# Around a one-slot expert stage: weights before squares, relu rows in buffers of their own, two conversions and one scale moved

## The chip, the core and the metric

The kernel runs on one core of a Trainium2 chip. The metric is the device time of one execution in microseconds (us). Five engines run side by side, each through its own instruction list in order: TensorE (PE, matrix products and transposes; PEld is its weight load), VectorE (DVE), ScalarE (ACT), GpSimd (POOL) and SyncE (SP, which here only issues DMAs). They wait for one another through semaphores.

## What is computed

Causal attention with a decay over 4 x 8 heads of 576 rows gives 2304 tokens of 512 numbers. Each token goes to one of eight experts (two matrices with a relu between), its row is scaled by a gate, and a dense layer pair with a softplus between follows for all tokens.

```
out[mask] = gate_w[mask, None] * (np.maximum(x[mask] @ w1[e], 0.0) @ w2[e])     # for each expert e
h = x @ w_in
g = np.maximum(h, 0.0) + np.log1p(np.exp(-np.abs(h)))
return g @ w_out
```

## The kernel before

After the attention (to about 240 us) and the routing (to about 280 us) come nine expert stages, in the order of `ORDER`: three-slot stages `t`, two-slot stages `b` and the only one-slot stage `s`. A slot is 128 token rows of one expert. The text numbers the stages 0 to 8; stage 5 is `("t", 1)`, **stage 6 is `("s", 0)`**, stages 7 and 8 are `("t", 2)` and `("t", 3)`. Then comes the dense layer pair (`ffn`).

**Weights.** A stage uses eight pieces of weights of 512 KB; W6[4] is piece 4 of stage 6. Pieces 0 to 3 serve the first product of a stage (L1149, in stage 6 L1219), 4 to 7 the second (L1129), whose eight blocks `fb` = 0 to 7 use one half piece each. `wsplit` handles a piece: an SP DMA into a buffer `raw` of the pool `stage` (four buffers in all), ACT writes the high part `wh` (L1040), DVE the low part `wl` (L1041). `feed(ph, want)` does one missing piece of the current stage, or, when that has all eight, pieces of the next stage until it has `want`. A DMA of a piece is issued when the `raw` that was handed out four before it has been read by DVE.

**Dense conversions.** `conv.step()` loads 512 KB of the dense weights through the same four `raw` buffers, in fixed order, and DVE turns them in three instructions (L1417 to L1419); an ACT square (L1426) follows later. The table `STEPS` says behind which of a stage's 16 blocks (eight of the first product, eight of the second) a step stands.

**Rows.** `xslot` makes the next stage's token columns: four PE transposes into one of two PSUM banks, ACT `xh` (L1086), DVE `xl` (L1087); in stage 6 it stands behind `fb` 1, 3 and 5 for the three slots of stage 7. At a stage's end `scatter` has ACT write the result row `y` (L1116, three buffers) and POOL scatter it by DMA; `square` (L1104, ACT) takes its sum of squares. In stage 6 (`small`) ACT writes relu rows `hs` (L1223), which before the change take a buffer of `y`; `turn` transposes `hs`, ACT writes `hh` (L1232) and DVE `hl` (L1233).

**The dense pair.** It goes over five chunks of rows, chunk 0 of 512 rows first, in 16 steps each; `n` counts all steps. In step n PE does the first product of step n and the second product of step n-3. DVE does `e`, `e` of step n-1, `r` and `u` of n, then `gl` of n-1 (L1542, L1543, L1528, L1530, L1549); POOL does one subtraction (L1531) between `u` and the next `e`. Behind odd n up to 13 one dense piece is split (ACT L1434, DVE L1435). In chunk 0 the scale of the later chunks is found: `total` (DVE, `y_m` and `y_mb`), `add` (one PE product, L1460), then `find` and `scale(1)` (nine small DVE instructions, L1464 to L1484). `rows.prep` makes the columns of chunk 1 with that scale: four PE transposes (L1378) into the only bank T, ACT high part, DVE low part (L1380).

Of the kernel before, what the change touches and what calls it, by code (L numbers as in the profile page):

```python
# [9 lines left out]
F32 = mybir.dt.float32  # L10
# [16 lines left out]
DM = H * D  # L27
# [8 lines left out]
ROWS = "tbs"  # L36
NG = 9
STEPS = {0: "0101010010101010", 1: "0001000001000000", 2: "0001000001000000", 3: "0001000001000000", 4: "0001000001000000",
         5: "0101010010101000", 7: "0101010010101000", 8: "1110110000000000"}
STEPS = {ph: [x == "1" for x in s] for ph, s in STEPS.items()}  # L40
SPLITS = [(0,), (1, 2), (3, 4), (5,), (6,), (7,), (), ()]
ORDER = [("t", 0), ("b", 0), ("b", 1), ("b", 2), ("b", 3), ("t", 1), ("s", 0), ("t", 2), ("t", 3)]
# [1 line left out]
NMAIN = len(SLOTS)  # L44
# [4 lines left out]
WROW = 528  # L49
# [839 lines left out]
def compact(tc, g, p, ps):  # L889
    nc = tc.nc  # L890
    V = nc.vector
    x = 0
    tok, flag = (p.tile([128, NMAIN], dt, name=nm, bufs=1) for nm, dt in (("ptok", F32), ("pflag", BF16)))
    kept = p.tile([128, NMAIN], F32, name="pkept", bufs=1)
    V.tensor_copy(g.tok, g.gidx)
    while x < NMAIN:
        m, y = SLOTS.index(PLACES[x]), 1
        while x + y < NMAIN and m + y < NMAIN and SLOTS[m + y] == PLACES[x + y]:
            y += 1
        V.tensor_copy(tok[:, x:x + y], g.tok[:, m:m + y])  # L900
        V.tensor_copy(kept[:, x:x + y], g.pv[:, 0, m:m + y])
        x += y
    V.scalar_tensor_tensor(flag, tok, float(KEPT), kept, op0=ALU.is_lt, op1=ALU.mult)
    V.tensor_tensor(kept, kept, flag, op=ALU.subtract)
    V.tensor_tensor(tok, tok, g.dmf, op=ALU.subtract)
    V.tensor_tensor(tok, tok, kept, op=ALU.mult)
    V.tensor_tensor(tok, tok, g.dmf, op=ALU.add)
    yield
    n = ps()[:, 0:NMAIN]
    nc.tensor.matmul(n, g.onesm, flag, start=True, stop=True)  # L910
    sums = p.tile([128, NMAIN], F32, name="sums", bufs=1)
    V.tensor_tensor_scan(sums, g.onesm[:, 0:NMAIN], n, 0.0, op0=ALU.mult, op1=ALU.add)
    first = p.tile([128, 1], F32, name="first", bufs=1)
    V.tensor_scalar(first, sums[:, NMAIN - 1:NMAIN], -1.0, float(KEPT), op0=ALU.mult, op1=ALU.add)
    V.tensor_tensor(sums, sums, n, op=ALU.subtract)
    V.tensor_scalar(sums, sums, g.row, first, op0=ALU.add, op1=ALU.add)
    V.tensor_tensor(sums, sums, g.dmf, op=ALU.subtract)
    V.tensor_tensor(sums, sums, flag, op=ALU.mult)
    V.tensor_tensor(g.sidx, sums, tok, op=ALU.add)
    a = p.tile([128, NMAIN], I32, name="batch", bufs=1)  # L920
    gate_rows(V, g.grow, g.gidx, a)
# [54 lines left out]
def experts(tc, g, w1, w2, win, wout, out):  # L976
# [4 lines left out]
    phases = list(ORDER)  # L981
    n_ph = len(phases)
    with ExitStack() as both, ExitStack() as ctx:
# [5 lines left out]
        yp = g.yp = pool("e_y", 3)  # L989
# [4 lines left out]
        hp = pool("e_h", 4, ctx)  # L994
# [137 lines left out]
        def wide(ph):  # L1132
            w = WIDTH[phases[ph][0]]
            n = 128 * w
            last = ph == n_ph - 1
            xh, xl = (t.rearrange("p c a n -> p c (a n)") for t in X.pop(ph))
            hts = []
            for gg in range(4):
                hh = hp.tile([128, 2, n], F32R, name="hh", tag="hh")
                hl = hp.tile([128, 2, n], F32R, name="hl", tag="hl")  # L1140
                if w == 2:
                    pair = ps_h.tile([128, 2, n], F32, name="h", tag="h")
                for a in range(2):
                    pl = pair[:, a] if w == 2 else ps_h.tile([128, n], F32, name="h", tag="h")
                    fs = slice(128 * (2 * gg + a), 128 * (2 * gg + a) + 128)
                    for c in range(4):
                        wh, wl = W[ph][c]
                        for m, (x, y) in enumerate(((wh, xh), (wh, xl), (wl, xh))):
                            nc.tensor.matmul(pl, x[:, fs], y[:, c], start=(c == 0 and m == 0),  # L1149
                                             stop=(c == 3 and m == 2))  # L1150
                    if w == 2 and a == 0:
                        continue
                    src, to = (pair, slice(0, 2)) if w == 2 else (pl, a)
                    nc.scalar.activation(hh[:, to], src, ACTF.Relu)
                    nc.vector.scalar_tensor_tensor(hl[:, to], src, 0.0, hh[:, to].bitcast(F32), op0=ALU.max, op1=ALU.subtract)
                    if 2 * gg + a in (0, 2, 6):
                        feed(ph, 0)
                    if STEPS[ph][2 * gg + a]:
                        conv.step()
                    if ph == 0 and (gg, a) == (0, 0):  # L1160
                        gates(tc, g, g.lt)
                    if ph == 0 and (gg, a) in ((1, 1), (3, 0)):
                        if gg == 1:
                            store_gates(tc, g, hp, bank)
                        next(places, None)
                hts += [(hh[:, a], hl[:, a]) for a in range(2)]
                if w == 2 or gg == 0:
                    feed(ph, 0)
                square()
                if gg == 0 and ph == n_ph - 2:  # L1170
                    conv.powers["i"].total(g.wsq[:, 0], ALU.add)
                if gg == 3 and last:
                    rows.powers[0].total(g.ysq, ALU.max)
            if last:
                for a in range(SIZES[0]):
                    rows.load(0, a)
            py = [ps_y.tile([128, DM], F32, name="y", tag="y") for _ in range(w)]
            for fb in range(8):
                l2(ph, py, hts[fb], fb, range(w))
                xnext(ph, fb)  # L1180
                if fb and not last:
                    feed(ph, min(fb, 4))
                if fb == 1:
                    ggather(ph)
                if not last and STEPS[ph][8 + fb]:
                    conv.step()
                if ph == n_ph - 2 and fb == 2:
                    conv.powers["i"].add(bank()[:, 0:1])
                if ph == n_ph - 2 and fb == 3:
                    conv.powers["i"].find()  # L1190
                if last:
                    if fb == 0:
                        conv.square(0)
                    if fb == 1:
                        conv.powers["o"].total(g.wsq[:, 1], ALU.add)
                    if fb == 2:
                        rows.powers[0].add(bank()[:, 0:1])
                        rows.powers[0].find()
                    if 3 <= fb < 3 + SIZES[0]:
                        rows.prep(0, fb - 3, bank)  # L1200
                    for x in SPLITS[fb]:
                        conv.split("i", x // 2, x % 2)
                    if fb == 5:
                        conv.powers["o"].add(bank()[:, 0:1])
                        conv.powers["o"].find()
                    if fb == 7:
                        conv.split("o", 0, 0)
            for a in range(w):
                scatter(ph, a, py[a])

        def small(ph, after1=None):
# [7 lines left out]
                    nc.tensor.matmul(pl, x[:, c], w[:, fs], start=(c == 0 and m == 0), stop=(c == 3 and m == 2))  # L1219

            def relu(pl):
                hs = yp.tile([128, WROW], F32, name="hs", tag="y")[:, 0:DM]
                nc.scalar.activation(hs, pl, ACTF.Relu)  # L1223
                return hs

# [16 lines left out]
            pl = ps_h.tile([128, 512], F32, name="h", tag="h")  # L1242
            for c in range(4):
                half_mm(pl, 0, c)
            while squares:
                square()
            h0 = relu(pl)
            next_weights(0)
            next_weights(0)
# [13 lines left out]
            for fb in range(8):  # L1263
                l2(ph, py, hts[fb], fb, [0])
                if fb == 0 and not after1:
                    hts += turn(h1)
                if main and fb % 2:
                    xnext(ph, fb // 2)
                if fb < 4:
                    next_weights(fb + 1)  # L1270
                if fb == 2 and main:
                    ggather(ph)
# [214 lines left out]
def ffn(tc, g, conv, rows, square, out):  # L1487
# [4 lines left out]
    with ExitStack() as ctx:  # L1492
# [91 lines left out]
        for n in range(len(units) + 3):  # L1584
# [14 lines left out]
                conv.split("o", *late[n])  # L1599
            if n < 3:  # L1600
                square()
            if n == 5:
                rows.powers[1].total(g.ysq, ALU.max)
            if n == 7:
                rows.powers[1].add(bank()[:, 0:1])
                rows.powers[1].find()
                scale(1)
            if n >= 3:
                l2(*units[n - 3])
            if n < len(units) and c + 1 < NC:  # L1610
                for a in range(SIZES[c + 1]):
                    if fb == (1 + 2 * a if c else (6, 7, 8, 11)[a]):
                        rows.load(c + 1, a)
                    if fb == (3 + 2 * a if c else (9, 11, 12, 14)[a]):
                        rows.prep(c + 1, a, bank)


# [33 lines left out]
```

## Time and profile before

| quantity | value |
|---|---|
| median of three runs | 915.23 us (914.03 to 915.61) |
| the profiled execution, its own time | 914.66 us |
| its span, first to last instruction | 912.9 us |
| mean granted TensorE clock | 0.981 |
| busy: PE, DVE, ACT, POOL | 858.8, 702.2, 565.0, 378.9 us |
| stage 5, stage 6, stages 7 and 8 begin on PE | 396.8, 430.3, 449.5, 486.9 us |
| dense pair begins on PE | 523.8 us |

The times in the text are of the profiled execution, counted from the start of its span; 1.8 us of its own time lie outside the span. PE is the busiest engine, but its matmul ends are modelled, so what counts is where it sat idle and what ended the idle time.

### The profile page before, as it was taken

To read this page: it belongs to the slowest core of one execution; us is meant where nothing else is said; L and a number is where in the kernel's file an instruction comes from. 1 tells how busy PE (TensorE), PEld (TensorE's weight loads), DVE (VectorE), ACT (ScalarE), POOL (GpSimd) and SP (SyncE) were. 2 spreads that over 40 slices of the span, in tenths; PEclk is the share of its full clock that TensorE was granted. 3 is DMA by queue.
4 is the path that set the end of the run, shared out by engine and by line. 5 is a ranking of instruction groups with operands and counts; after the bars stand their busy time and mean duration, and the time that the engine had idled before them with its cause. 6 is when DMAs were issued, how large, how long until landed. Compare 5 with 4: busy or idle time off the path is not lost.

```text
span 912.9 us, 17317 instructions
## 1 busy us (share of the span) xinstructions
PE 858.8 (94%) x6298; PEld 595.7 (65%) x6298; DVE 702.2 (77%) x1541; ACT 565.0 (62%) x1052; POOL 378.9 (42%) x526
## 2 busy tenths in 40 slices
PE   2999999999649999999799999999999999999998
PEld 2888787887539998898598844444444444664443
DVE  3788888888678777776587867888878778777775
ACT  3788888788564666665655776655454554566453
POOL 6678677777252322423403043324222422334221
PEclk9999999999859999999999999999999999999999
DMA  8776676691336878887767120101100200100001
GB/s 179 160 164 146 153 161 146 147 244 42 105 98 210 287 274 270 261 302 258 258 201 271 51 71 1 33 16 59 32 5 1 70 1 1 59 1 24 1 1 46
DMA packets 102814, 109.72 MB, mean 120 GB/s; under 512 B 62948, under 2 KB 72184, under 8 KB 102720
## 3 DMA queue, kind: packets, MB, share of 16 engines
q1 hardware_dynamic: 97282, 93.49, 36.4%
q0 software_dynamic: 5152, 14.87, 4.6%
q8 instruction: 51, 0.84, 0.4%
q14 instruction: 43, 0.35, 0.1%
q10 hardware_dynamic: 286, 0.17, 0.1%
HBM read 93.31 MB, written 15.20 MB: 119 GB/s over the span
## 4 chain that ended last, share of the span: by engine, by line
PE 52%; DVE 8%; POOL 3%; DMA 3%; ACT 3%; issue 2%; DVEq 0%; POOLq 0%; ACTq 0%
PE h L1517 14%; PE y L1562 11%; PE h L1149 11%; PE y L1129 10%; PE t L1562 4%; POOL e L1531 2%; DMA raw<-in_moe_w_dram 2%; DVE r L1528 2%; DVE e L1542 2%; DVE wl L1041 1%; DVE e L1543 1%; PE t L1085 1%; DVE dw L1435 1%; DVE u L1530 1%; ACT wh L1040 1%
## 5 line engine op out<-in xcount | busy, mean ns | idle before, releaser
L1531 POOL TENSOR_TENSOR e<-u,e 128x512 f32<-128x512 f32 (+1 forms) x80 | 103.8, 1297 | 245.2 <-DVE u L1530 241.9
L1527 ACT ACTIVATE e<-h,s_h 128x512 f32<-128x512 f32 (+1 forms) x80 | 51.2, 640 | 122.8 <-PE h L1517 122.7
L1562 PE MATMUL y<-dw,gh 128*128 128x512 f16 x448 | 111.4, 379 | 0.7 <-ACT ob L1570 0.7
L1549 DVE SCALAR_TENSOR_TENSOR gl<-e,s_gup,gh 128x512 f16<-128x512 f32 (+1 forms) x80 | 97.4, 1218 | 9.1 <-ACT gh L1547 8.7
L1562 PEld LDWEIGHTS <-gh 128*128 128x128 f16 x576 | 56.3, 98 | 66.2 <-ACT e L1529 1.0
L1041 DVE TENSOR_TENSOR wl<-raw,wh 128x1024 fp32r<-128x1024 f32 x64 | 77.8, 1223 | 21.3 <-ACT wh L1040 20.2
L1149 PE MATMUL h<-xh,wh 128*128 128x384 f32 (+1 forms) x256 | 80.3, 314 | 4.5 <-ACT xh L1086 3.3
L1149 PE MATMUL h<-xl,wh 128*128 128x384 f32 (+1 forms) x256 | 79.8, 312 | 0.9 <-DVE xl L1087 0.9
L1149 PE MATMUL h<-xh,wl 128*128 128x384 f32 (+1 forms) x256 | 79.9, 312 | 0.7 <-DVE wl L1041 0.7
L1528 DVE TENSOR_SCALAR r<-h,s_h 128x512 f32<-128x512 f32 (+1 forms) x80 | 55.6, 695 | 32.3 <-ACT e L1527 32.2
L1040 ACT ACTIVATE wh<-raw 128x1024 fp32r<-128x1024 f32 x64 | 67.0, 1055 | 21.5 <-DMA raw<-in_moe_w_dram 20.3
L339 DVE SCALAR_TENSOR_TENSOR pts<-pt,pts 128x512 f16<-128x512 f32 (+3 forms) x128 | 69.8, 567 | 11.9 <-ACT pts L336 11.2
L1517 PEld LDWEIGHTS <-wh 128*128 128x128 f16 x480 | 47.2, 99 | 47.4 <-issue 1.4
L1517 PEld LDWEIGHTS <-wl 128*128 128x128 f16 x480 | 47.1, 98 | 46.9 <-issue 0.8
L1547 ACT ACTIVATE gh<-e,s_gup 128x512 f16<-128x512 f32 (+1 forms) x80 | 53.6, 670 | 34.4 <-DVE e L1543 34.4
L336 ACT ACTIVATE pts<-pt 128x512 f16<-128x512 f32 (+3 forms) x128 | 58.5, 496 | 23.2 <-PE pt L349 11.1
L1129 PE MATMUL y<-wh,hh 128*128 128x512 f32 x168 | 67.8, 404 | 0.3 <-ACT hh L1232 0.3
L1542 DVE TENSOR_TENSOR e<-r,e 128x512 f32<-128x512 f32 (+1 forms) x80 | 50.4, 630 | 22.8 <-POOL e L1531 22.8
L313 ACT ACTIVATE p<-sm,mx 128x512 f32<-128x512 f32 (+3 forms) x128 | 67.9, 559 | 0.0
L1517 PE MATMUL h<-yth,wh 128*128 128x512 f16 x192 | 65.9, 384 | 0.0
L1129 PE MATMUL y<-wl,hh 128*128 128x512 f32 x168 | 65.7, 391 | 0.0
L1517 PE MATMUL h<-yth,wl 128*128 128x512 f16 x192 | 65.2, 380 | 0.0
(343 smaller groups left out, 2413.0 us busy)
## 6 DMA issues: line engine op xcount, KB each, us to landing
raw<-in_moe_w_dram SPq DMA_DIRECT2D x68, 512.0 KB
cb<-ncum SPq DMA_DIRECT2D x32, 288.0 KB
raw<-in_moe_w_in_dram SPq DMA_DIRECT2D x16, 512.0 KB
raw<-in_moe_w_out_dram SPq DMA_DIRECT2D x16, 512.0 KB
yg<-yd SPq DMA_DIRECT2D x18, 264.0 KB
cb<-ncum SPq DMA_DIRECT2D x32, 144.0 KB
qt<-in_q_dram SPq DMA_DIRECT2D x32, 128.0 KB
kt<-in_k_dram SPq DMA_DIRECT2D x32, 128.0 KB
```

The lines of the kernel that those rows point to most:

```text
L313: nc.scalar.activation(p[:, 0:n], s[:, 0:n], ACTF.Exp, scale=-1.0, bias=m)
L339: nc.vector.scalar_tensor_tensor(lo, ps, UP, hi, op0=ALU.mult, op1=ALU.subtract)
L1040: nc.scalar.activation(hi, r, ACTF.Copy)
L1041: nc.vector.tensor_sub(lo, r, hi.bitcast(F32))
L1129: nc.tensor.matmul(py[a], x[:, 128 * a:128 * a + 128], w[:, fb % 2], start=(fb == 0 and m == 0 and w is wh), stop=(fb == 7 and m == 1))
L1149: nc.tensor.matmul(pl, x[:, fs], y[:, c], start=(c == 0 and m == 0), stop=(c == 3 and m == 2))
L1517: nc.tensor.matmul(pl, w[:, fs], x[:, d], start=(d == 0 and m == 0), stop=(d == 3 and m == 2))
L1528: nc.vector.tensor_scalar(r, pl, back, 0.0, op0=ALU.mult, op1=ALU.max)
L1531: nc.gpsimd.tensor_sub(e, u, e)
L1542: nc.vector.tensor_sub(d, r, d)
L1549: nc.vector.scalar_tensor_tensor(gl, d, s, gh, op0=ALU.mult, op1=ALU.subtract)
L1562: nc.tensor.matmul(PO[c][a], x, w, start=(fb == 0 and m == 0 and w is wh), stop=(fb == FB - 1 and m == 1))
```

## The change

In stage 5 `feed` may go to six pieces of stage 6 instead of four, so W6[4] and W6[5] are split behind blocks 5 and 6 of stage 5, two blocks after W6[3]. In stage 6 `hs` gets two buffers of its own, and the three squares of stage 5's rows move from ahead of the first relu to behind blocks 5, 6 and 7. Of the dense conversions one leaves stage 5 (block 4 of its second product); stage 7 gets two more, behind the last two blocks of its second product; stage 8 has four (behind blocks 1, 3, 4 and 5 of its first product) where it had five (0, 1, 2, 4, 5). In the dense pair `total` moves from step 5 to 4, `add`, `find` and `scale(1)` from step 7 to 8, and the first `prep` of chunk 1 from step 9 to 10. `sums` reuses the tile `kept`.

```diff
 STEPS = {0: "0101010010101010", 1: "0001000001000000", 2: "0001000001000000", 3: "0001000001000000", 4: "0001000001000000",
-         5: "0101010010101000", 7: "0101010010101000", 8: "1110110000000000"}
+         5: "0101010010100000", 7: "0101010010101011", 8: "0101110000000000"}
...
-    sums = p.tile([128, NMAIN], F32, name="sums", bufs=1)
+    sums = kept
...
                 if fb and not last:
-                    feed(ph, min(fb, 4))
+                    feed(ph, min(fb, 6 if phases[ph + 1][0] == "s" else 4))
...
             def relu(pl):
-                hs = yp.tile([128, WROW], F32, name="hs", tag="y")[:, 0:DM]
+                hs = hp.tile([128, DM], F32, name="hs", tag="hs", bufs=2)
...
-            while squares:
-                square()
+            if not main:
+                while squares:
+                    square()
...
+                if main and fb > 4:
+                    square()
...
-            if n == 5:
+            if n == 4:
                 rows.powers[1].total(g.ysq, ALU.max)
-            if n == 7:
+            if n == 8:
                 rows.powers[1].add(bank()[:, 0:1])
                 rows.powers[1].find()
                 scale(1)
...
-                    if fb == (3 + 2 * a if c else (9, 11, 12, 14)[a]):
+                    if fb == (3 + 2 * a if c else (10, 11, 12, 14)[a]):
                         rows.prep(c + 1, a, bank)
```

The first place is ACT from the end of stage 5 to the end of stage 6 (`wh` is a weight piece, `y` and `junk,ysq` the result rows and their squares, `hs` the relu rows). Before:

```order
L1116 ACTIVATE y<-y,gsl 128x512 x3
L1104 ACTIVATE junk,ysq<-y 128x512 x3
L1223 ACTIVATE hs<-h 128x512
L1040 ACTIVATE wh<-raw 128x1024 x2
L1232 ACTIVATE hh<-t 128x512
L1040 ACTIVATE wh<-raw 128x1024
L1223 ACTIVATE hs<-h 128x512
L1040 ACTIVATE wh<-raw 128x1024
L1232 ACTIVATE hh<-t 128x512
L1040 ACTIVATE wh<-raw 128x1024
L1086 ACTIVATE xh<-t 128x4x128
```

And of the change, the same place:

```order
L1040 ACTIVATE wh<-raw 128x1024 x6
L1116 ACTIVATE y<-y,gsl 128x512 x3
L1223 ACTIVATE hs<-h 128x512
L1040 ACTIVATE wh<-raw 128x1024 x2
L1232 ACTIVATE hh<-t 128x512
L1223 ACTIVATE hs<-h 128x512
L1232 ACTIVATE hh<-t 128x512
L1040 ACTIVATE wh<-raw 128x1024
L1086 ACTIVATE xh<-t 128x4x128
...
L1104 ACTIVATE junk,ysq<-y 128x512 x3
```

Two `wh` have moved from between the relu rows to ahead of the `y` rows (six in a row now), and the three squares from ahead of the first `hs` to the end of the stage. DVE's `wl` and SP's DMAs move with the `wh`.

The second place is DVE at the border of stages 7 and 8 (`wl` a weight piece, `dw` a dense conversion of three instructions, `hl` the low part of a first product). Before, from the last `wl` of stage 7:

```order
L1041 TENSOR_TENSOR wl<-raw,wh 128x1024
L1417 TENSOR_SCALAR dw<-raw 128x512
L1418 SCALAR_TENSOR_TENSOR dw<-raw,dw 128x512
L1419 SCALAR_TENSOR_TENSOR dw<-raw,dw 128x512
L1155 SCALAR_TENSOR_TENSOR hl<-h,hh 128x384
L1041 TENSOR_TENSOR wl<-raw,wh 128x1024
L1417 TENSOR_SCALAR dw<-raw 128x512
L1418 SCALAR_TENSOR_TENSOR dw<-raw,dw 128x512
L1419 SCALAR_TENSOR_TENSOR dw<-raw,dw 128x512
L1155 SCALAR_TENSOR_TENSOR hl<-h,hh 128x384
L1417 TENSOR_SCALAR dw<-raw 128x512
```

And of the change (the lines below the edit bear numbers three higher):

```order
L1422 SCALAR_TENSOR_TENSOR dw<-raw,dw 128x512
L1420 TENSOR_SCALAR dw<-raw 128x512
L1421 SCALAR_TENSOR_TENSOR dw<-raw,dw 128x512
L1422 SCALAR_TENSOR_TENSOR dw<-raw,dw 128x512
L1420 TENSOR_SCALAR dw<-raw 128x512
L1421 SCALAR_TENSOR_TENSOR dw<-raw,dw 128x512
L1422 SCALAR_TENSOR_TENSOR dw<-raw,dw 128x512
L1155 SCALAR_TENSOR_TENSOR hl<-h,hh 128x384
L1041 TENSOR_TENSOR wl<-raw,wh 128x1024
L1155 SCALAR_TENSOR_TENSOR hl<-h,hh 128x384
L1420 TENSOR_SCALAR dw<-raw 128x512
```

Three conversions now stand ahead of the first `hl` of stage 8, where one stood, and none between its first and second `hl`, where one stood.

The third place is DVE in the dense pair, steps 7 and 8 of chunk 0 (`gl` closes a step; `y_b` to `s_o` are `find` and `scale(1)`; the `dw` split stands in odd steps). Before, the end of step 7:

```order
L1528 TENSOR_SCALAR r<-h,s_h 128x512
L1530 TENSOR_SCALAR u<-e 128x512
L1549 SCALAR_TENSOR_TENSOR gl<-e,s_gup,gh 128x512
L1435 SCALAR_TENSOR_TENSOR dw<-dw,o_up 128x1024
L1464 TENSOR_SCALAR y_b<-t 128x1
...
L1484 TENSOR_TENSOR s_o<-s_gdn,o_dn 128x1
L1542 TENSOR_TENSOR e<-r,e 128x512
```

And of the change, from the end of step 7 through step 8:

```order
L1552 SCALAR_TENSOR_TENSOR gl<-e,s_gup,gh 128x512
L1438 SCALAR_TENSOR_TENSOR dw<-dw,o_up 128x1024
L1545 TENSOR_TENSOR e<-r,e 128x512
L1546 TENSOR_TENSOR e<-e,v 128x512
L1531 TENSOR_SCALAR r<-h,s_h 128x512
L1533 TENSOR_SCALAR u<-e 128x512
L1552 SCALAR_TENSOR_TENSOR gl<-e,s_gup,gh 128x512
L1467 TENSOR_SCALAR y_b<-t 128x1
...
L1487 TENSOR_TENSOR s_o<-s_gdn,o_dn 128x1
L1545 TENSOR_TENSOR e<-r,e 128x512
```

The nine small instructions have moved from behind a split to behind the `gl` of a step without a split; `total` moves in the same way from step 5 to step 4.

## Rows read from the trace of the kernel before

**Rows 1.** PE's list of waits from stage 5 on: total, times, longest.
```profile
PE h L1149 <- DVE hl L1155: 1.0, 1, 1.0
...
PE t L1460 <- DVE y_mb L1456: 0.7, 1, 0.7
PE y L1562 <- ACT ob L1570: 0.7, 1, 0.7
```

**Rows 2.** Stretches: window, its length, busy by engine, granted clock, DMA.
```profile
451.10:454.50 3.40, 3.40 (x12) 3.40 (x12) 0.00 (x0) 0.00 (x0) 2.62 (x3) 0.50 0.86 322
...
587.60:591.00 3.40, 3.40 (x12) 1.42 (x10) 2.75 (x6) 1.93 (x3) 1.36 (x1) 0.50 0.02 6
```

**Rows 3.** PE timeline in stages 6 and 7: start, duration, idle before.
```profile
432.81 0.39 PE L1219 MATMUL h<-wh,xl 128*128 128x512 f32 x1
...
439.06 0.50 PE L1129 MATMUL y<-wh,hl 128*128 128x512 f32 x1 [0.83 <-DVE hl L1233]
...
449.48 0.44 PE L1149 MATMUL h<-xh,wh 128*128 128x384 f32 x1 [3.30 <-ACT xh L1086]
450.85 0.51 PE L1149 MATMUL h<-xl,wh 128*128 128x384 f32 x1 [0.93 <-DVE xl L1087]
```

**Rows 4.** ACT timeline in stage 6.
```profile
433.35 0.63 ACT L1104 ACTIVATE junk<-y 128x512 bf16<-128x512 f32 x1
...
434.47 0.60 ACT L1223 ACTIVATE hs<-h 128x512 f32<-128x512 f32 x1 [0.39 <-DMA yd<-y,sidx]
434.96 2.00 ACT L1040 ACTIVATE wh<-raw 128x1024 fp32r<-128x1024 f32 x2
...
445.59 1.06 ACT L1040 ACTIVATE wh<-raw 128x1024 fp32r<-128x1024 f32 x1 [1.44 <-DMA raw<-in_moe_w_dram]
```

**Rows 5.** DVE timeline in stage 6.
```profile
436.04 2.36 DVE L1041 TENSOR_TENSOR wl<-raw,wh 128x1024 fp32r<-128x1024 f32 x2 [6.80 <-ACT wh L1040]
...
450.11 0.68 DVE L1087 TENSOR_TENSOR xl<-t,xh 128x512 fp32r<-128x512 f32 x1
```

**Rows 6.** SP's DMA issues: W6[4] to W6[7], then W7[0] to W7[3].
```profile
423.40 6.24 SPq L1021 DMA_DIRECT2D raw<-in_moe_w_dram  x4
437.30 4.33 SPq L1018 DMA_DIRECT2D raw<-in_moe_w_dram  x4
```

**Rows 7.** DVE timeline at the start of stage 8.
```profile
489.74 0.56 DVE L1155 SCALAR_TENSOR_TENSOR hl<-h,hh 128x384 fp32r<-128x384 f32 x1 [4.00 <-ACT hh L1154]
...
498.62 0.42 DVE L1417 TENSOR_SCALAR dw<-raw 128x512 uint32<-128x512 uint32 x1
...
500.41 1.02 DVE L1155 SCALAR_TENSOR_TENSOR hl<-h,hh 128x384 fp32r<-128x384 f32 x2
```

**Rows 8.** DVE timeline in the dense pair, chunk 0.
```profile
549.93 0.69 DVE L1542 TENSOR_TENSOR e<-r,e 128x512 f32<-128x512 f32 x1 [1.17 <-POOL e L1531]
...
555.59 0.16 DVE L1456 CAST y_mb<-y_m 128x1 bf16<-128x1 f32 x1
...
565.31 0.15 DVE L1464 TENSOR_SCALAR y_b<-t 128x1 int32<-128x1 int32 x1
...
565.75 0.16 DVE L1478 TENSOR_TENSOR s_h<-y_dn,i_dn 128x1 f32<-128x1 f32 x1
...
566.52 0.68 DVE L1542 TENSOR_TENSOR e<-r,e 128x512 f32<-128x512 f32 x1
...
586.49 0.74 DVE L1380 SCALAR_TENSOR_TENSOR wl<-t,y_up,wh 128x512 f16<-128x512 f32 x1
```

**Rows 9.** PE timeline in the dense pair: third prep of chunk 1.
```profile
587.29 0.86 PE L1378 MATMUL t<-ident,yg 128*128 128x128 f32 x4 [1.94 <-DVE wl L1380]
```

**Rows 10.** POOL timeline in the dense pair.
```profile
594.15 1.28 POOL L1531 TENSOR_TENSOR e<-u,e 128x512 f32<-128x512 f32 x1 [2.68 <-DVE u L1530]
```

**Rows 11.** DVE timeline beside it.
```profile
589.47 0.75 DVE L1549 SCALAR_TENSOR_TENSOR gl<-e,s_gup,gh 128x512 f16<-128x512 f32 x1
...
594.25 1.72 DVE L1549 SCALAR_TENSOR_TENSOR gl<-e,s_gup,gh 128x512 f16<-128x512 f32 x1 [0.18 <-ACT gh L1547]
```

## The prediction

> **What bounds the kernel now.** I read four views: the list of PE's waits, to see where PE sits still; the windows, for the clock that it was granted there; the timelines of PE, ACT and DVE around each wait, for what was late; and SP's issues, for when a weight piece was asked for. From stage 5 on PE waits in few places: before the second product of stage 6, at the start of stage 7, once in stage 8, twice in chunk 0 of the dense pair, and after that once, for 0.7 us [rows 1, 3, 9]. So behind 591 us PE is full, and what it gains before that moves the end by as much. The sum goes by PE.
>
> Two of the waits cost twice. Behind the idle time at the start of stage 7 PE is granted 0.50 of its clock (its lower level) from 451.1 to 454.5, and behind the 1.94 us that end at 587.29 again for 3.4 us [rows 2, 3, 9]: half of 3.4, 1.7 us of work each. The 1.0 us wait of stage 8 has no such row behind it.
>
> **Stage 6 into stage 7: 3.9 us.** At the start of stage 7 PE has `xh` at 449.48 and its second product only at 450.85, when `xl` of the third slot is there [rows 3]. That `xl` is the end of a queue: DVE does four pieces of stage 6 and four of stage 7, five other low parts between, at 1.15 us a piece (two in 2.36, overlapping a little) and 0.6 to 0.7 a low part [rows 5]. It begins only at 436.04, since ACT comes to the first piece at 434.96, behind three squares (0.63 us and a read of the sum each, 0.75 together) and a relu that waits 0.39 us for the scatter of a `y` buffer [rows 4, 5]. The last pieces are late for the same reason: W7[0] is asked for at 437.30, when DVE has freed the `raw` of W6[4], and ACT then waits 1.44 us for W7[2] [rows 4, 6].
>
> The change takes the squares and the scatter out of ACT's way. The first half product's last matmul starts at 432.81 [rows 3], so I put the relu at 433.25 instead of 434.47 and the next two pieces, now W6[6] and W6[7], at 433.85 to 435.85. DVE follows: `wl` to 436.05 and 437.2, `hl` to 437.9. PE's third product of block 0, at 439.06 [rows 3], comes at 437.95, 1.1 us earlier. W6[4] and W6[5] are gone from here, two pieces of DVE and ACT each. From there ACT: after the transposes `hh` to 439.45, W7[0] to 440.4, `xh`, W7[1] to 441.9, W7[2] to 442.9, `xh`, W7[3] to 444.4, `xh` to 445.0. DVE, in its order: `wl` 441.6, `xl` 442.2, `wl` 443.35 and 444.5, `xl` 445.1, `wl` 446.25, `xl` 446.9. Stage 7's second product starts at 446.95 instead of 450.85: **3.9 us**. PE ended stage 6 at 446.2 (449.48 less 3.30) and now does at about 445.1; it runs stage 7's first product and then waits some 1.5 us for DVE, which is what is late next. At nothing saved this term is 0; without any wait it is 5.3 us. I take 3.9, by the queue.
>
> Do the loads keep up? W6[4] to W6[7] are asked for from 423.40 on, some 2 us apart [rows 6]; one conversion's issue fewer stands before them, so each is about 2 us earlier. W7[0] and W7[1] follow when DVE has read W6[4] and W6[5], near 430 and 431, and land while the queues hold little but scatters. W7[2] and W7[3] are asked for at 436.05 and 437.2. Before, W7[2] was issued at about 440, two loads ahead of it, and was there at 445.59 [rows 4, 6]: 5.6 us. At 5.6 they come at 441.7 and 442.8, ahead of the 441.9 and 443.4 at which ACT is free.
>
> **What is moved without a price.** The added pieces cost ACT 1.0 and DVE 1.15 each, under the second product of stage 5, where nobody waits for either; uncovered up to 2.3, less the conversion of 1.8 that leaves (498.62 to 500.41, [rows 7]). The squares land between the last `xh` at 445.0 and stage 7's first relu, which stands behind twelve products from 446.95 on; uncovered 2.3 on ACT. `y` of stage 6 waits behind them, and POOL's scatter for that, but that row is read only for the dense pair. `hs` in new buffers and `sums` in an old one add no instruction.
>
> **Stage 8: 1.0 us.** DVE idles 4.00 us before stage 8's first `hl` and is then so full that PE waits 1.0 us for a PSUM bank, which the `hl` at 500.41 should free [rows 1, 7]. Two conversions, 3.6 us, move into that idle time; ahead of that `hl` stand two fewer, and the one added behind it has its slack to lie in. Bounds: 0, if the moved loads come late and DVE stands before them, and the 1.0; I take 1.0, since one conversion less would do. On SP their two DMAs go ahead of W8[4], which then waits for a buffer that is freed no later than before.
>
> **Dense pair: 2.1 us, and 1.7 of the clock.** PE comes to `add` 0.7 us before `y_mb`, which ends at 555.75, behind a split [rows 1, 8]. One step earlier `total` lies in a gap like the 1.17 us in which DVE waits for POOL [rows 8], near 549, and `add` comes a step later: the 0.7 goes. Then PE comes to the third prep at 585.35 and waits 1.94 us for the bank, which the second prep's DVE part frees at 587.23 [rows 8, 9]. Of what holds DVE up till then, `total` (about 0.3, two such instructions) and the nine small ones (565.31 to 566.52, 1.2) move from behind splits into such gaps, and the first prep's DVE part, 0.74 like the second's, moves beside POOL's work: DVE is some 2.1 us earlier there, at 585.1. PE is 0.7 earlier, at 584.6. About 0.5 of the 2.64 us remains: **2.1**. With no idle time near 2 us in one piece, the clock should not fall: **1.7** more. Bounds: 0.7 (`add` alone, the fall stays) and 4.3.
>
> DVE and POOL get in each other's way here: `gl` takes 0.75 us, but 1.72 where it starts behind POOL's subtraction, and then ends half a microsecond behind that one's end [rows 10, 11]. "SBUF — State Buffer" in the Trainium skill, section "Who interferes with whom", has an exclusive lock between a GpSimd operation that reads SBUF and a VectorE one with two SBUF inputs. This trace agrees with it. By that rule the two-input ones of the nine would stand still in their new gap until POOL ends, and about 1.3 in place of 2.1 would be gained.
>
> **Sum.** 3.9 + 1.0 + 2.1 + 1.7 = 8.7 us off the profiled execution's 914.66: **906.0 us**. That execution is 0.6 under the median of the runs, inside their spread.
>
> **Rivals.** *The clock holds at the start of stage 7.* I count its fall as coming back, since some 1.5 us of idle time is nearer to the 1.94 that brought one than to the 1.0 that did not. If it holds, 1.7 more: 904.3. For it speaks that PE's idle time there was 4.2 us and is cut to less than half.
>
> *The small instructions wait for POOL*, as that `gl` does [rows 10, 11]. The first that reads two SBUF tiles is `s_h`; from it to the next `e` are 0.8 us (565.75 to 566.52, [rows 8]). They would come back onto DVE's path: 0.8 back, 906.8. No row has one of them beside a running subtraction.
>
> *The one bank holds the preps up.* They now stand in steps 10, 11 and 12 without a gap, and each needs the bank of the one before. If DVE is early by only half of the 2.1 us, PE waits 1.6 in all, and the clock falls again: 1.1 + 1.7 back, 908.8.
>
> *Slower.* The two extra pieces stand in ACT's order ahead of stage 5's `y` rows and the first relu. If W6[5] lands after 432.2 (the relu's 433.25 less one `wh`), each us delays the relu, and with it all of stage 6, by one. It is asked for at about 423.4; the slow W7[2] took 5.6 us, so 429 is what the rows say. Landing at 440.9 would eat the whole 8.7; from 442.7 on the kernel is over 0.2% slower, 916.5 or more.
>
> *The change does nothing*: what stages 6 and 8 gain is eaten by a wait behind them, loads of stage 7 that come late for stage 8, and the dense pair keeps its fall: about 914. Against it: in stage 7's products PE has no wait at all in the list [rows 1].
>
> **Numbers.** Chances: forecast 0.42 (904.9 to 907.4 by its own bounds), clock holds 0.26, POOL 0.12, bank 0.10, nothing 0.07, slower 0.03. Range 903.0 to 910.0: it takes in the first four, and leaves some of what lies beyond them. A measurement here tells 0.2%, 1.8 us, from no change. Faster by more are the first four, 0.89 with a little off; same 0.07; slower 0.04.
>
> **What would show it.** Right: no wait for `hs`; `xl` at stage 7's start still ends a wait, but at 447; no wait of PE in stage 8's first product, none at `y_mb`, under 1 us at the preps, the granted clock whole behind them. Wrong: ACT waiting for a `raw` before stage 5's `y` rows, PE waiting in stage 7's or 8's products for `wl`, or a prep that waits over 1.5 us.

## The result and the profile after

The changed kernel takes 903.44 us (median of 4 runs, 902.01 to 905.5), the kernel before 915.18 beside it: a ratio of 0.9875, with a 95% interval of 0.9854 to 0.9897. The forecast was 906.0 us, in a range of 903.0 to 910.0: right in sign, 2.6 us short in size. The profiled execution takes 903.77, with a span of 902.0; against the 914.66 of before that is 10.9 us, where the sum had 8.7.

PE's list of waits from stage 5 on, after (total, times, longest), answers to [rows 1]. Of nine entries four are left; lines below L1270 have moved down by 3.

```profile
PE h L1149 <- DVE xl L1087: 1.6, 1, 1.6
PE t L1381 <- DVE wl L1383: 1.1, 2, 0.9
PE y L1129 <- DVE hl L1233: 0.8, 1, 0.8
PE y L1565 <- ACT ob L1573: 0.7, 1, 0.7
```

ACT around the start of stage 6, after ([rows 4]):

```profile
427.70 1.06 ACT L1040 ACTIVATE wh<-raw 128x1024 fp32r<-128x1024 f32 x1 [2.30 <-DMA raw<-in_moe_w_dram]
429.15 1.06 ACT L1040 ACTIVATE wh<-raw 128x1024 fp32r<-128x1024 f32 x1 [0.39 <-DMA raw<-in_moe_w_dram]
430.12 1.83 ACT L1116 ACTIVATE y<-y,gsl 128x512 f32<-128x512 f32 x3
432.79 0.60 ACT L1223 ACTIVATE hs<-h 128x512 f32<-128x512 f32 x1 [0.83 <-PE h L1219]
```

The first two are W6[4] and W6[5]; each waits for its load. That is one of the signs that the prediction named for being wrong (ACT waiting for a `raw` before stage 5's `y` rows), but here it cost nothing: the rows `y` follow at 430.12, as before the change at 430.11, and the relu `hs` waits for nothing but PE's products. The queue that it starts, on DVE, after ([rows 5]):

```profile
434.36 2.36 DVE L1041 TENSOR_TENSOR wl<-raw,wh 128x1024 fp32r<-128x1024 f32 x2 [2.88 <-ACT wh L1040]
436.64 0.68 DVE L1233 TENSOR_TENSOR hl<-t,hh 128x512 fp32r<-128x512 f32 x1
439.00 0.69 DVE L1233 TENSOR_TENSOR hl<-t,hh 128x512 fp32r<-128x512 f32 x1 [1.67 <-ACT hh L1232]
...
444.55 1.22 DVE L1041 TENSOR_TENSOR wl<-raw,wh 128x1024 fp32r<-128x1024 f32 x1
445.68 0.69 DVE L1087 TENSOR_TENSOR xl<-t,xh 128x512 fp32r<-128x512 f32 x1
```

And PE at its end, after ([rows 3]):

```profile
437.38 0.51 PE L1129 MATMUL y<-wh,hl 128*128 128x512 f32 x1 [0.83 <-DVE hl L1233]
...
444.42 0.44 PE L1149 MATMUL h<-xh,wh 128*128 128x384 f32 x1
446.43 0.44 PE L1149 MATMUL h<-xl,wh 128*128 128x384 f32 x1 [1.56 <-DVE xl L1087]
```

Stage 7's second product comes at 446.43 instead of 450.85. Stage 6 itself began 0.44 us earlier in this execution, so 3.98 of the 4.42 lie between stage 6's first product and stage 7's second. One wait of 1.56 us remains, and the clock behind it is whole, as it is behind the preps of the dense pair (windows, after, against [rows 2]; the column before the last two is the granted clock):

```profile
446.43:449.83 3.40, 3.40 (x19) 3.40 (x20) 0.56 (x1) 1.81 (x4) 1.68 (x2) 1.00 0.98 325
572.03:575.43 3.40, 3.40 (x18) 1.86 (x19) 2.90 (x5) 2.23 (x4) 1.05 (x1) 1.00 0.32 84
```

In the dense pair PE's waits are now these, for the bank that the first and then the second prep held ([rows 9]):

```profile
572.03 0.66 PE L1381 MATMUL t<-ident,yg 128*128 128x128 f32 x4 [0.92 <-DVE wl L1383]
...
578.04 0.65 PE L1381 MATMUL t<-ident,yg 128*128 128x128 f32 x4 [0.17 <-DVE wl L1383]
```

and on DVE the small instructions, in their new gap ([rows 8]):

```profile
560.54 0.14 DVE L1469 TENSOR_SCALAR y_dn<-y_b 128x1 int32<-128x1 int32 x1
560.71 0.80 DVE L1481 TENSOR_TENSOR s_h<-y_dn,i_dn 128x1 f32<-128x1 f32 x1
561.44 0.15 DVE L1482 TENSOR_TENSOR s_z<-y_b,i_b 128x1 f32<-128x1 int32 x1
...
562.13 0.69 DVE L1545 TENSOR_TENSOR e<-r,e 128x512 f32<-128x512 f32 x1
```

POOL's subtraction beside them ([rows 10]):

```profile
559.78 1.72 POOL L1534 TENSOR_TENSOR e<-u,e 128x512 f32<-128x512 f32 x1 [3.64 <-DVE u L1533]
```

`s_h`, 0.16 us before, takes 0.80 and ends at 561.51; POOL ends at 561.50.

### The profile page after: what moved, and what is told of

It reads as the page before. It is cut to its first block, busy times and chain, and to the rows that moved or that the text cites. A ratio compares the mean times of both kernels' runs of the same rounds, so it can differ in the third digit from the quotient of the medians.

```text
span 902.0 us, 17320 instructions
## 1 busy us (share of the span) xinstructions
PE 854.6 (95%) x6298; PEld 593.3 (66%) x6298; DVE 701.0 (78%) x1541; ACT 564.9 (63%) x1052; POOL 384.0 (43%) x526
## 4 chain that ended last, share of the span: by engine, by line
PE 54%; DVE 8%; ACT 3%; POOL 3%; issue 2%; DMA 1%; DVEq 0%; POOLq 0%; ACTq 0%
PE h L1520 14%; PE h L1149 12%; PE y L1565 11%; PE y L1129 10%; PE t L1565 4%; POOL e L1534 2%; DVE r L1531 2%; DVE e L1545 2%; DVE wl L1041 1%; ACT wh L1040 1%; DMA raw<-in_moe_w_dram 1%; DVE e L1546 1%; PE t L1085 1%; DVE dw L1438 1%; DVE u L1533 1%
```

## The experiments

Runs of one kernel differ by several us, more than most parts are worth. The profiles tell where: stage 6 begins between 427.98 and 432.02 us in them, with no order by kernel, and PE's clock falls in some executions and not in others. So each profile is read by PE's own stretches, start to start: from stage 6's first product to stage 7's second, from there to stage 8's first, from there to the dense pair's first, and from there to the last product of the program. Each figure is a difference of two starts in PE's timeline; brackets say where the clock fell in the stretch. The falls in the stretches of 36.06 and 384.71 last 3.4 to 3.5 us, those in 37.00 and 37.20 last 6.9.

```
kernel                        6 to 7      7 to 8      8 to dense  dense to end   sum
before                        20.54       36.06 [fell] 36.91      384.71 [fell]  478.22
after                         16.56       34.46        35.20      381.53         467.75
after, again                  16.54       34.46        35.20      381.44         467.64
stage 6 edits alone           16.75       34.49        36.96      383.00         471.20
conversions alone             19.90       36.06 [fell] 35.18      383.00         474.14
dense edits alone             19.84       37.00 [fell] 36.90      381.41         475.15
no early pieces               19.49       37.20 [fell] 36.95      382.99         476.63
early pieces alone            23.62 [fell] 34.49       36.90      382.99         478.00
early pieces, own hs buffers  19.60 [fell] 34.47       36.93      383.01         474.01
scalar form, s_h and s_o      16.56       34.45        35.20      381.46         467.67
scalar form, all three        16.61       36.06 [fell] 35.84      381.00         469.51
W7[3] late                    15.41       34.46        35.20      381.45         466.52
three edits more              14.43       34.49        35.19      381.01         465.12
W7[3] and W7[2] late          13.65       35.35        35.24      380.93         465.17
```

**The parts, each alone.** First the edits around stage 6: early pieces, own buffers, squares behind the slots (`sums` in the tile `kept` goes with every kernel that has the own buffers).

```
-                    feed(ph, min(fb, 4))
+                    feed(ph, min(fb, 6 if phases[ph + 1][0] == "s" else 4))
...
-                hs = yp.tile([128, WROW], F32, name="hs", tag="y")[:, 0:DM]
+                hs = hp.tile([128, DM], F32, name="hs", tag="hs", bufs=2)
...
-            while squares:
-                square()
+            if not main:
+                while squares:
+                    square()
...
+                if main and fb > 4:
+                    square()
```

> The edits around stage 6 alone (six pieces taken early, relu rows in buffers of their own, squares behind the last slots); conversions and dense pair as before. Theory (the after trace read as a queue on DVE): the second product of stage 7 comes 4.0 us earlier, and the clock does not fall behind its wait, which gives 1.7 more; the fall behind the third prep at 587 stays, since its 1.94 us wait stays. So 5.6 us off 915.2: 909.6. Rival, as the prediction had it: the fall at the start of stage 7 comes back, 911.3. Second rival: the fall at 587 goes with the one at 451, 907.9.

Measured: 908.28 (ratio 0.9937, 0.9918 to 0.9955). The stretch into stage 7 is 16.75, as in the changed kernel, and the clock does not fall at 451. It does not fall behind the third prep in this profile either, though the 1.94 us wait stands there. The median lies between the theory and the second rival; of its six runs two have a mean clock of 0.981, four 0.983 or more.

The conversions alone:

```
-         5: "0101010010101000", 7: "0101010010101000", 8: "1110110000000000"}
+         5: "0101010010100000", 7: "0101010010101011", 8: "0101110000000000"}
```

> The moved conversions alone. Theory: the 1.0 us in which PE waits in stage 8 for the bank goes and nothing takes its place, both clock falls stay: 914.2. Rival: the stretch of the after trace hides other gains (its stages 6 and 7 end earlier and their loads with them), and alone the conversions wait for their loads: 915.2, no change.

Measured: 911.26 (0.9968, 0.9954 to 0.9982). Stage 8 gives 1.73 us here (36.91 to 35.18), as much as in the changed kernel, and not 1.0; neither theory had that. PE's timeline of the kernel before shows why:

```profile
497.16 0.34 PE L1149 MATMUL h<-xh,wl 128*128 128x384 f32 x1
497.62 0.44 PE L1149 MATMUL h<-xh,wh 128*128 128x384 f32 x1
...
499.66 0.34 PE L1149 MATMUL h<-xh,wl 128*128 128x384 f32 x1
501.01 0.44 PE L1149 MATMUL h<-xh,wh 128*128 128x384 f32 x1 [1.01 <-DVE hl L1155]
```

Products follow each other at 0.17 us here. The one behind the wait starts 1.35 us after its predecessor, so the wait listed as 1.01 costs 1.18; and a short stop at 497.62, which no list has, costs 0.29 more. The next product behind each of the two stops comes after 0.28 us, 0.11 more than usual. That makes 1.69 of the 1.73, all of it in the stage's first product; from the second product's start to its last matmul the two kernels take the same 18.51 us.

The dense edits alone:

```
-            if n == 5:
+            if n == 4:
                 rows.powers[1].total(g.ysq, ALU.max)
-            if n == 7:
+            if n == 8:
...
-                    if fb == (3 + 2 * a if c else (9, 11, 12, 14)[a]):
+                    if fb == (3 + 2 * a if c else (10, 11, 12, 14)[a]):
```

> The edits of the dense pair alone (total in step 4, find in step 8, first prep in step 10). Theory: as in the after trace 0.7 us at add goes, and of 1.94 us at the preps 1.1 remains in two pieces, with no fall of the clock behind them: 1.5 + 1.7 off, 912.0, with the fall at 451 still there. Rival: the fall at 587 depends on more than that one wait and stays: 913.6.

Measured: 911.84 (0.9973, 0.9958 to 0.9989). From the dense pair on 381.41 us, against 383.00 in the five profiles that have the old dense part and no fall there: 1.59 from the edits. The fall at the start of stage 7 is there, as the theory had it, and the one behind the third prep is not; but over the twelve runs the mean clock is 0.9807, against 0.9802 in the runs of before, so the runs don't show that the edits bring the 1.7 us of that fall back.

The three medians lie 6.1, 3.1 and 2.5 below the 914.37 of before: 11.7 together, as much as the whole change gave at first, and more than the 9.9 that it gave when measured again (below). Each is known to 1.3 to 1.7 us, so this shows no large effect of the parts on each other, and could not show a small one.

**Inside the stage 6 part.** The same edits without the early pieces (`feed(ph, min(fb, 4))` as before):

> As the first of these, but with four pieces taken early as before: W6[4] and W6[5] are converted inside stage 6 still. Theory (a queue on DVE from its first piece to the last xl): the queue starts 1.7 us earlier, since ACT comes to its first piece behind one relu rather than behind three squares, and still holds eight pieces, so the second product of stage 7 comes 1.7 us earlier; PE still idles over 3 us at that place and the clock still falls: 913.5. Rival: the squares and the hs buffers are the whole gain, and the two early pieces are worth nothing: 909.6, as with them.

Measured: 913.84, no difference (0.999, 0.9977 to 1.0002). The stretch into stage 7 is 19.49, 1.05 less than the profile of before and 0.35 less than the dense edits alone, which have the code of before up to there. Both theories were too generous. The queue on DVE starts 1.2 us earlier, counted from stage 6's first product, but ACT then waits for loads, four times; this is the last, W7[3]:

```profile
447.73 1.06 ACT L1040 ACTIVATE wh<-raw 128x1024 fp32r<-128x1024 f32 x1 [1.85 <-DMA raw<-in_moe_w_dram]
```

SP could ask for W7[0] to W7[3] only from 436.96 on, 5.8 us behind stage 6's first product, as `raw` buffers came free (SP's issues in the same kernel):

```profile
436.96 4.34 SPq L1018 DMA_DIRECT2D raw<-in_moe_w_dram  x4
```

and in the changed kernel from 430.05, 0.2 us behind it, since W6[4] and W6[5] were done in stage 5:

```profile
430.05 7.04 SPq L1018 DMA_DIRECT2D raw<-in_moe_w_dram  x4
```

So the early pieces free the buffers 5.6 us sooner. How much of their worth is that, and how much the work taken off DVE, was not tried apart: without them DVE stands idle 2.4 us ahead of the last three pieces of stage 7 (0.30, 0.51 and 1.56), and this kernel is 2.7 us behind the stage 6 edits into stage 7, but its queue holds two pieces more as well.

The other half, early pieces alone in the kernel before:

> The kernel before with six pieces taken early and nothing else: the three squares and the scatter's buffer still stand in ACT's way. Theory (the loads of stage 7 are what held the queue up: with W6[4] and W6[5] converted in stage 5 their buffers come free 7 us sooner): most of the 4.0 us of both edits, 2.8, comes from here, with PE's idle time at stage 7 still near 2.5 us and the clock falling or not: 911.5 with the fall, 909.5 without. Rival (the three squares and the scatter start the queue 1.7 us late, and that counts here too): 1.7 or less, 913 or more.

Measured: 913.88, no difference (0.9999, 0.9982 to 1.0015), and the stretch into stage 7 is 3.1 us longer. The theory fell: here is ACT.

```profile
431.27 1.06 ACT L1040 ACTIVATE wh<-raw 128x1024 fp32r<-128x1024 f32 x1 [0.27 <-DMA raw<-in_moe_w_dram]
432.23 1.83 ACT L1116 ACTIVATE y<-y,gsl 128x512 f32<-128x512 f32 x3
433.94 0.64 ACT L1104 ACTIVATE junk<-y 128x512 bf16<-128x512 f32 x1
...
439.48 0.60 ACT L1223 ACTIVATE hs<-h 128x512 f32<-128x512 f32 x1 [3.31 <-DMA yd<-y,sidx]
```

W6[5] is there only at 431.27, 1.1 us behind stage 6's first product (in the changed kernel 0.7 ahead of it), so `y` starts at 432.23 and not at 430.11, its scatter leaves later, and the relu, which takes a buffer of `y`, waits 3.31 us for it behind three squares. PE waits 5.8 us for `hs`. That is the mechanism of the prediction's *slower* rival. The changed kernel is spared it by the buffers and the moved squares, and in its profile also by a load that came earlier. With the relu rows in buffers of their own, but the squares still in front (the two edits `feed` and `hs`):

> The kernel before with six pieces taken early and the relu rows in buffers of their own; the three squares stay ahead of the first relu. Measure: from stage 6's first product to stage 7's second, 20.5 us before, 16.6 with all three edits, 23.6 with six early pieces alone. Theory (there ACT comes to the relu late twice: behind three squares, 2.25 us, and then by the scatter of the y buffer, 3.3): without the scatter the relu comes 3.3 earlier, so 20.3, no gain over before by that measure; 914. Rival (the scatter was the whole delay, the squares lie under PE's second half products): 16.6 to 17.5, 910.5.

Measured: 910.74 (0.9967, 0.9948 to 0.9985). The relu comes at 436.26, counted from stage 6's first product 3.6 earlier, where the theory had 3.3; 19.60 into stage 7, 0.7 better than it said, and again no fall of the clock at the start of stage 7, only one behind the 2.1 us that PE still waits for `hs`. The time is the rival's, but not in the rival's way: by the profiles 0.9 us come from the stretch and 1.6 from the fall at stage 7 that this one lacks. Of the 6.1 us of the three edits, then, early pieces alone give nothing, buffers and squares 0.5, which is not clear of nothing, early pieces and buffers 2.4. Early pieces with the squares moved, and the buffers or the squares alone, were not run. One edit frees the loads, one takes the scatter and one the squares out of ACT's way.

**The small instructions and POOL.** In the changed kernel, `s_h` and `s_o` as a tensor times a per-partition scalar:

```
-        V.tensor_tensor(self.h, y.dn, i.dn, op=ALU.mult)
+        V.tensor_scalar(self.h, y.dn, i.dn, None, op0=ALU.mult)
...
-        V.tensor_tensor(self.o, dn.bitcast(F32), o.dn, op=ALU.mult)
+        V.tensor_scalar(self.o, dn.bitcast(F32), o.dn, None, op0=ALU.mult)
```

> The changed kernel (903.4), with s_h and s_o written as a tensor times a per-partition scalar, so that they read one tensor each; s_z stays a sum of two tensors. Theory (an instruction of DVE that reads two SBUF tensors waits for POOL's running subtraction): s_h is back at 0.16 us, and s_z, the next one with two tensors, waits in its place and ends with POOL as s_h did; no gain, 903.4. Rival 1 (only what reads the new y scale was slow, or the first instruction behind a chain of small ones): s_z stays at 0.15, 0.65 us gained, 902.8. Rival 2 (any second operand from SBUF waits, a scalar too): s_h stays at 0.80, 903.4.

Measured: 903.81. DVE in this kernel:

```profile
559.39 0.21 DVE L1481 TENSOR_SCALAR s_h<-y_dn,i_dn 128x1 f32<-128x1 f32 x1
559.52 0.67 DVE L1482 TENSOR_TENSOR s_z<-y_b,i_b 128x1 f32<-128x1 int32 x1
```

`s_h` no longer waits, and the next instruction with two tensors does, until 560.19, where POOL ends at 560.16 (558.45 and 1.71). Both rivals fell. With `s_z` in the same form:

```
-        V.tensor_tensor(z, y.b, i.b, op=ALU.add)
+        V.tensor_scalar(z, y.b, i.bf, None, op0=ALU.add)
```

> As the one before with s_z in the same form too, its operand put into float once, ahead of step 0 (one more instruction of 0.15 us there). Theory (two SBUF tensors wait for POOL): none of the nine takes over 0.2 us, the next e starts when POOL ends, and PE's wait at the preps falls from 1.1 to about 0.5: 902.8. Rival (what is saved on DVE is lost at e, which waits for POOL's result in any case): the next e starts no more than 0.1 earlier and PE waits 1.1 still: 903.4.

Measured: 902.89. DVE:

```profile
563.63 0.21 DVE L1481 TENSOR_SCALAR s_h<-y_dn,i_dn 128x1 f32<-128x1 f32 x1
563.76 0.20 DVE L1482 TENSOR_SCALAR s_z<-y_b,i_bf 128x1 f32<-128x1 int32 x1
...
564.57 0.68 DVE L1545 TENSOR_TENSOR e<-r,e 128x512 f32<-128x512 f32 x1
```

POOL ends at 564.40 here (562.69 and 1.71), and `e` follows 0.17 behind instead of 0.63. PE waits 0.43 and 0.17 at the preps, and from the dense pair on it takes 381.00 instead of 381.53. (The 35.84 ahead of that hold a wait of 0.5 us for `ytl` at a scale's `add`, which no other profile has.) The theory's 0.6 comes out as 0.5 in the profile; the medians, under 1 us apart, say nothing on it. This profile also shows a fall behind `xl` at the start of stage 7, which the changed kernel's two profiles don't have (window, granted clock third from the end):

```profile
448.10:451.30 3.20, 3.20 (x11) 3.20 (x11) 0.52 (x1) 1.04 (x2) 2.31 (x3) 0.50 1.00 370
```

**Towards a faster version.** W7[3] converted behind the last `xl`:

```
-                if fb < 4:
-                    next_weights(fb + 1)
+                if fb < 3 or fb == 5:
+                    next_weights(min(fb + 1, 4))
```

> The changed kernel (903.4) with piece W7[3] converted behind the third slot's xl rather than ahead of it. Theory (the last xl is the end of DVE's queue, and one piece of 1.15 us stands needlessly ahead of it): the second product of stage 7 comes 1.15 us earlier and PE's wait there falls from 1.6 to 0.4: 902.2. Rival: PE needs wl of W7[3] in that first group and waits for it instead, or ACT's xh comes no earlier: 903.4.

Measured: 902.49; stage 7's second product comes 15.41 after stage 6's first instead of 16.56, the 1.15 forecast, and waits 0.61. With that, the scalar form, and W6[7] converted behind the first `turn`:

```
             next_weights(0)
-            next_weights(0)
...
             hts += turn(h0)
             next_weights(0)
+            next_weights(0)
```

> The changed kernel with three edits more: W7[3] converted behind the last xl, the three small sums and products of the dense scales written with one tensor each, and W6[7] converted behind the transposes of h0 (so that one piece rather than two stands ahead of the first hl). Theory (each of PE's waits is its own, and behind the pair PE is full): 1.0 from W7[3], 0.5 from the small instructions, 0.7 at the first hl: 901.2. Rival (DVE's queue between the slots only hands the wait on: what W6[7] leaves, it takes back at the second hl or at the last xl): 901.9.

Measured: 900.25 (5 runs, 898.99 to 901.73; 0.9852 of before, 0.9836 to 0.9867), the fastest version, 4.3 us under the changed kernel beside it. From 16.56 to 14.43 into stage 7 and 0.5 in the dense pair are 2.6 us by the profiles. The rest is not shown to be theirs: stage 6 began at 427.98 in this profile and at 430.99 in the other. PE's waits in this kernel:

```profile
PE y L1565 <- ACT ob L1573: 0.7, 1, 0.7
PE h L1149 <- DVE xl L1087: 0.6, 1, 0.6
PE t L1381 <- DVE wl L1383: 0.6, 2, 0.4
```

The changed kernel beside it:

> The changed kernel once more, beside the one above, for its own spread. Theory: 903.4 as measured, with no fall of the clock between 440 and 600 us in any profile, so a mean clock of 0.983 to 0.985 in every run. Rival (the falls come and go from run to run, and the first runs were lucky): some of its runs at 0.979 to 0.981, and 1 to 2 us longer.

Measured: 904.51, 9.9 under the 914.44 of before beside it (0.9902, 0.9884 to 0.992). No fall between 440 and 600 us in the profile; but two of its six runs have a mean clock of 0.981 and 0.982, and these are its longest, 907.78 and 905.58. The rival is partly right.

Last, W7[2] behind the last `xl` as well, and the squares behind both:

```
-                if fb < 3 or fb == 5:
+                if fb < 2 or fb == 5:
                     next_weights(min(fb + 1, 4))
+                if fb == 5:
+                    next_weights(4)
```

> The version with three edits more (900.25), with W7[2] converted behind the last xl as well, and the squares behind both pieces. Theory (the last xl is still the end of DVE's queue, PE waits 0.6 for it): that wait goes, and wl of W7[2] is there 1.2 us behind the last xl, as late as PE's seventh product wants it: 899.7. Rival (the stop moves into the group of twelve products: PE waits for wh or wl of W7[2] or W7[3] by as much): 900.3, or up to a microsecond more.

Measured: 901.57. The wait at `xl` goes (13.65) and comes back inside the group of twelve (35.35 to stage 8 instead of 34.49). PE in this kernel:

```profile
447.61 0.33 PE L1149 MATMUL h<-xl,wh 128*128 128x384 f32 x1
448.29 0.44 PE L1149 MATMUL h<-xh,wl 128*128 128x384 f32 x1 [0.35 <-DVE wl L1041]
```

The sums are 465.17 and 465.12: the rival was right, nothing gained. DVE's work ahead of stage 7 can be put in another order, but at that point no longer hidden.

## Why the prediction came out as it did

**Stage 6 into stage 7, 3.9 us: right by its steps, and in size within the spread of before.** 3.98 measured against the profile that the prediction was read from. The dense edits alone, with the code of before up to there, take 19.84 and not 20.54, with ACT waiting 0.82 and 0.53 us for the last two loads and not 1.44 and 0.75: against that profile it is 3.3. The relu was put at 433.25 and PE's third product at 437.95; with stage 6's own start 0.44 earlier they came at 433.23 and 437.82. The last `xl` let PE go on at 446.87 by the same clock, forecast 446.95. The 1.5 us of wait left are 1.56. The loads were on time, as worked out. What the prediction did not see is how the edits depend on each other: it costed the early pieces as time of ACT and DVE, and mentioned the freed buffers only to show that the loads would keep up.

**The clock at the start of stage 7: the step that failed.** The prediction counted that fall as coming back, since "some 1.5 us of idle time is nearer to the 1.94 that brought one than to the 1.0 that did not". The rival held: 36.06 to 34.46, 1.60 more. The reading behind the step was wrong: one row in one execution was taken as what 1.94 us does. In the profiles of all these kernels a wait of 1.5 to 1.95 us on PE, at `xl` or at a prep, stands twelve times from stage 5 on, with a fall behind it in two; one of 2.1 us or more six times, each with a fall in it or behind it, and in four of the six a second wait of 0.7 to 1.2 us follows 1.4 to 1.7 us later. Waits of up to 1.2 us that don't follow such a long one have none.

**The clock behind 587 us, 1.7: right between the two profiles (1.71), and that by luck.** Five kernels with the old preps keep the 1.94 us wait and show no fall in their profiles, so the term is the same wrong reading as the one before: the profile that was read happened to have this fall. Over all runs: in 74 runs of the kernel before the mean granted clock is 0.9802 on average, in ten of the changed kernel 0.9833. That is 0.0031 of 912 us, or 2.8 us of work, where the two profiles have 3.3. By the parts' runs most of it comes from the other place: the stage 6 edits alone have 0.9825, 0.0023 or 2.1 us above before, the dense edits alone 0.0005 or 0.5 us. So the prediction counted the clock where the runs show little and left it out where they show more. Runs of the kernel before at 0.983 average 912.4, at 0.981 913.7, at 0.979 915.3 and at 0.977 916.0: their time goes with the clock, though where it fell in them is not on record.

**Stage 8, 1.0: right place, mis-sized term; it measured 1.71.** The wait was costed by its idle time in the list, 1.0, and not by the delay of the product behind it; and a shorter stop was in no list.

**Dense pair, 2.1: mis-sized; it measured 1.5 to 1.6.** The 0.7 at `add` went, and of the 1.94 at the preps 1.1 remained, not 0.5. The step that failed is that the nine small instructions cost nothing in a gap beside POOL: the rival had it, at 0.8, and taking the second tensors away gave 0.5 back. The Trainium skill, "SBUF — State Buffer", section "Who interferes with whom", has this as a rule: a VectorE instruction with two SBUF inputs contends with a GpSimd one that reads SBUF, for a lock that only one of them holds. This case agrees, with `s_h` at 0.80 and, in its turn, `s_z` at 0.67; by that rule the prediction said 1.3. The bank did hold the preps up, 1.1 us in two pieces where the prediction had set under 1 as its sign, without a fall.

**The sum.** 3.98 + 1.60 + 1.71 + 1.71 + 1.47 make 10.47, the difference of the two sums in the table, and 0.44 is the earlier start of stage 6: 10.9. Against the forecast's 8.7 that is 1.6 for the clock, 0.7 for stage 8 and 0.4 for the start, less 0.6 in the dense pair. The start is not explained by the change: the profile of the changed kernel taken again begins stage 6 at 430.99, later than before.

## What to carry to other kernels

Early work also frees the buffers that later loads wait for: try it together with whatever else blocks the queue, since each half alone may show nothing. Price a wait by the start of the instruction behind it against its normal pace, and a clock fall by several executions, never by one. Before small VectorE work goes into a gap beside GpSimd, give it one tensor input and take the second operand as a per-partition scalar.

## What the runs showed of the hardware that was not expected

- A 128x1 sum or product on VectorE with two SBUF tensors took 0.67 to 0.80 us beside a GpSimd subtraction, ending within 0.03 us of it, and 0.15 to 0.16 without one; with a per-partition scalar as second operand it took 0.20 to 0.21 beside the same subtraction.
- The granted clock fell to its lower level behind a wait of 1.7 to 1.94 us in some executions and not in others with the same instructions: behind `xl`, 1.73 brought a fall in one kernel's profile and none in another's.
- Seven profiles of kernels that are the same up to stage 6 reached it between 427.98 and 432.02 us. Part of that is the clock long before: between 239 and 275 us the granted clock was 0.57 in the three that began stage 6 at 429.87, 430.99 and 432.02, and 0.62 in the four that began it between 427.98 and 430.51. In both groups PE had the lower level for most of that window, for some 3.4 us longer in the first. What sets the rest was not tried.
